# Loading batches 1 and 2 of q and k in 72 token runs: attention and a low-rank mixer on one Trainium2 core

## The chip, the cores and the metric

The kernel runs on one core of a Trainium2 chip. The metric is the time of one execution on the device in microseconds (us). Before the change the median of 8 executions is 364.96 us, the lowest 364.33, the highest 365.54.

## What is computed

Eight batches of eight heads, 576 tokens, 64 numbers per head. Attention is causal, with a bias from the running sum of a gate `s`; its output, heads side by side (512 wide), goes through a mixer over tokens of rank 32 and a two-layer network with a hidden width of 2048.

```python
scores = scale * np.matmul(q, k.transpose(0, 1, 3, 2))
s_pos = np.maximum(s, 0.0)
cum = np.cumsum(s_pos, axis=-1)
bias = -(cum[:, :, :, None] - cum[:, :, None, :])
scores = np.where(causal, -1000000000.0, scores + np.minimum(bias, 0.0))
attn = softmax(scores)
x = heads_side_by_side(np.matmul(attn, v))
u = x + (x.transpose(0, 2, 1) @ U @ V).transpose(0, 2, 1)
out = u + np.maximum(u @ w_ch1, 0.0) @ w_ch2
```

(The softmax and the joining of heads are shortened here to a name.)

## The kernel before

Work on q and k goes by pairs of heads. There are 32 pairs, four to a batch: pair n belongs to batch n // 4, so pairs 4 to 7 are batch 1 and pairs 8 to 11 batch 2. For each batch `alloc_qk` gives two tiles, `q_sd` and `k_sd`, each with 72 partitions, 8 heads and 8 x 64 numbers per head; the pool keeps two of each. `load_qk(b, h, n)` issues two loads, q and then k, for n heads from head h. They go out on POOL's queue, q0 in the profile, since they turn float32 into bf16 on the way.

The 576 tokens of a head are 72 x 8, and there are two ways to lay them over 72 partitions. In the first (L117) partition p holds tokens 8p to 8p + 7, so each partition and head is one run of 2 KB in memory. In the second (L112) partition p holds tokens p, p + 72, p + 144 and so on, so each token's 256 bytes are a run of their own. `in_runs(b, h)` chooses: true means the second.

`transposes(n)` then turns each head with eight matmuls against an identity (L315), two tokens' worth of 64 numbers at a time, into a PSUM tile `pwork` of bf16. Four copies per pair bring it to a `slot`, two per head: one for the even and one for the odd of each two. In the second layout a copy writes 72 neighbouring tokens at a time (L335). In the first it writes every second number, and reads PSUM with its last two dims swapped (L338). `copies` puts most of these copies on DVE; on ACT are all those of one head of pairs 4, 8 and 9, among others. The scores of pair n (`scores`, L402, with exponentials at L417, L428, L434 on ACT) read the slot; the values (`values`, L462, followed by L471 and L472 on DVE) read the exponentials and v.

The order of the work is written by hand. PE and POOL run in program order throughout (`in_program_order`); DVE, ACT and SP do so up to the end of batch 0, and behind that the order that the tile framework gives them holds. POOL's order at the start is: loads of batch 0, masks and constants, v of batch 0 in a form of its own, U and V, the first half of w1; the masks of pair 0; `load_qk(1, 0, 4)`; memsets; masks of pair 1; the second half of w1; masks of pairs 2 and 3; `load_qk(1, 4, 4)`; the first half of w2; v of batch 1 in five parts (L186); the second half of w2; q and k of batch 2 in two halves; v of batch 2; q and k of batch 3 whole, and so on. Batch 0 is loaded two heads at a time.

On PE, pairs 4 to 9 are woven together with the feed-forward matmuls of the first 512 tokens: L648 multiplies by w1, L658 by w2. In this string T is a step of `transposes`, S of `scores`, V of `values`, M of the mixer, F a step of the feed-forward alone:

```python
    weave("S5 T6 S5 F T6 S5 F S5 S6 T7 S6 T7 S6 S6")
    weave("V4 V4 S7 V5 S7 V5 S7 V6 S7 V6 T8 T8 V7 S8 V7 S8 T9 S8 T9")
```

The softmax here doesn't subtract the row's maximum and nothing guards it: scores larger than these inputs give would overflow.

## Time and profile before

| what | us |
|---|---|
| median of 8 executions | 364.96 |
| the profiled execution | 365.3 |
| its span, first to last instruction | 363.6 |
| PE busy in 35 to 80 us | 44.08 of 45 |
| L338 copies: DVE 29, ACT 11 | 23.3 busy on DVE |
| L112 issues on POOL, heads 4-7 of batch 2 | 1.42 and 1.40 each |
| L117 issues on POOL | 0.69 to 0.82 each |

The engines are PE (matmuls; PEld its weight loads), DVE, ACT, POOL and SP. A row of the profile gives line, engine, operation, tiles written and read, count, busy time, mean duration in ns, and the idle time before with what ended it. The strip of 40 digits shows the busy share of each fortieth of the span in tenths. q0 is the queue of the DMAs that POOL issues. [...]

### The profile page before, as it was taken

To read this page: it belongs to the slowest core of one execution; us is meant where nothing else is said; L and a number is where in the kernel's file an instruction comes from. 1 tells how busy PE (TensorE), PEld (TensorE's weight loads), DVE (VectorE), ACT (ScalarE), POOL (GpSimd) and SP (SyncE) were. 2 spreads that over 40 slices of the span, in tenths; PEclk is the share of its full clock that TensorE was granted. 3 is DMA by queue.
4 is the path that set the end of the run, shared out by engine and by line. 5 is a ranking of instruction groups with operands and counts; after the bars stand their busy time and mean duration, and the time that the engine had idled before them with its cause. 6 is when DMAs were issued, how large, how long until landed. Compare 5 with 4: busy or idle time off the path is not lost.

```text
span 363.6 us, 9585 instructions
## 1 busy us (share of the span) xinstructions
PE 351.4 (97%) x3989; PEld 255.2 (70%) x4031; DVE 278.5 (77%) x607; ACT 209.6 (58%) x319; POOL 85.0 (23%) x108
## 2 busy tenths in 40 slices
PE   7999999999999999999999999999999999999995
PEld 3676566666688667876688667876688468678884
DVE  7866776779798758995699659975899279676976
ACT  3884985746763678347843676357835641565710
POOL 8988452514040403140214012000000000000000
PEclk9999999999999999999999999999999999999999
DMA  7999999999999899989993999461013401500063
GB/s 102 171 202 198 165 182 102 153 144 131 112 61 101 137 143 60 99 92 125 127 99 66 144 134 90 50 165 23 18 49 88 96 18 32 147 0 31 29 117 116
DMA packets 153027, 37.41 MB, mean 103 GB/s; under 512 B 136600, under 2 KB 151352, under 8 KB 152984
## 3 DMA queue, kind: packets, MB, share of 16 engines
q0 software_dynamic: 110016, 18.50, 81.8%
q1 hardware_dynamic: 42680, 18.11, 28.9%
q8 instruction: 31, 0.51, 0.6%
q10 hardware_dynamic: 288, 0.20, 0.2%
q14 instruction: 12, 0.10, 0.1%
HBM read 37.25 MB, written 9.70 MB: 129 GB/s over the span
## 4 chain that ended last, share of the span: by engine, by line
PE 75%; DVE 12%; ACT 6%; issue 3%; DMA 2%; SPq 1%; DVEq 0%; ACTq 0%
PE pwork L648 24%; PE pwork L693 20%; PE pscore L402 9%; PE pwork L462 7%; PE parts L853 3%; PE pwork L315 3%; PE pwork L658 3%; DVE slot L675 2%; ACT hT L929 2%; DVE o_sb L707 2%; DVE uT L516 2%; ACT pT L417 2%; DMA slot<-hT 2%; PE pscore L648 1%; DVE slot L338 1%
## 5 line engine op out<-in xcount | busy, mean ns | idle before, releaser
L648 PE MATMUL pwork<-uT,w_sb 128*128 128x512 bf16 x431 | 113.8, 379 | 2.1 <-ACT hT L929 0.5
L417 ACT ACTIVATE pT<-pscore 128x1024 bf16<-128x1024 f32 x56 | 57.2, 1030 | 55.6 <-PE pscore L402 54.7
L929 ACT ACTIVATE hT<-pwork 128x512 bf16<-128x512 f32 x108 | 65.2, 609 | 31.2 <-PE pwork L648 31.1
L648 PEld LDWEIGHTS <-w_sb 128*128 128x128 bf16 x480 | 41.3, 98 | 37.3 <-issue 0.7
L402 PE MATMUL pscore<-slot 68*128 68x320 bf16 (+1 forms) x500 | 56.0, 246 | 0.7 <-DMA slot<-hT 0.5
L402 PEld LDWEIGHTS <-slot 68*128 68x128 bf16 x564 | 41.2, 97 | 17.5 <-issue 1.3
L693 PEld LDWEIGHTS <-hT 128*128 128x128 bf16 x496 | 46.1, 98 | 7.2 <-issue 0.7
L186 POOL DMA_DIRECT2D v_slot<-in_v_dram x36 | 30.3, 856 | 78.5 <-PE pwork L462 70.1
L693 PE MATMUL pwork<-w_sb,hT 128*128 128x256 bf16 x384 | 48.2, 273 | 0.0
L347 DVE TENSOR_TENSOR pT<-pT,keep 128x512 bf16<-128x512 bf16 (+1 forms) x81 | 28.6, 353 | 21.0 <-ACT pT L417 14.8
L335 DVE COPY slot<-pwork 64x576 bf16<-64x576 bf16 x76 | 34.4, 453 | 4.7 <-PE pwork L315 3.9
L462 PEld LDWEIGHTS <-pT 128*128 128x128 bf16 x870 | 32.4, 97 | 5.3 <-issue 0.6
L462 PE MATMUL pwork<-v_slot,pT 128*128 128x65 bf16 x870 | 35.5, 193 | 0.2 <-DVE uT L516 0.2
L693 PE MATMUL pwork<-w_sum,slot 128*128 128x256 bf16 x256 | 32.0, 273 | 0.8 <-DVE o_sb L707 0.7
L472 DVE TENSOR_TENSOR x_sb<-pwork,rec 128x320 bf16<-128x320 f32 x64 | 31.2, 488 | 1.3
L428 ACT ACTIVATE pT<-pscore 128x1024 bf16<-128x1024 f32 x29 | 30.2, 1042 | 2.6 <-PE pscore L402 2.4
L471 DVE RECIPROCAL rec<-pwork 128x5 f32<-128x5 f32 x64 | 12.1, 190 | 20.4 <-PE pwork L462 20.0
L338 DVE COPY slot<-pwork 64x576 bf16<-64x576 bf16 x29 | 23.3, 802 | 5.3 <-PE pwork L315 3.5
L693 PEld LDWEIGHTS <-slot 128*128 128x128 bf16 x256 | 24.1, 98 | 4.5 <-issue 1.6
L112 POOL DMA_DIRECT2D q_sd<-in_q_dram x6 | 12.6, 2105 | 47.6 <-PE pwork L315 42.2
L707 DVE TENSOR_TENSOR o_sb<-o_sb,pwork 128x512 f32<-128x512 f32 (+2 forms) x34 | 21.9, 648 | 0.7 <-PE pwork L693 0.3
L315 PEld LDWEIGHTS <-q_sd 72*128 72x128 bf16 x256 | 14.9, 97 | 8.9 <-DMA q_sd<-in_q_dram 1.1
(161 smaller groups left out, 500.1 us busy)
## 6 DMA issues: line engine op xcount, KB each, us to landing
out_dram<-o_sb SPq DMA_DIRECT2D x35, 256.0 KB
w_sb<-in_moe_w_ch_dram POOLq DMA_DIRECT2D x4, 1024.0 KB, 12.2
v_slot<-in_v_dram POOLq DMA_DIRECT2D x28, 128.0 KB, 6.7
q_sd<-in_q_dram POOLq DMA_DIRECT2D x5, 576.0 KB, 13.7
k_sd<-in_k_dram POOLq DMA_DIRECT2D x5, 576.0 KB, 17.9
q_sd<-in_q_dram POOLq DMA_DIRECT2D x4, 288.0 KB, 12.6
k_sd<-in_k_dram POOLq DMA_DIRECT2D x4, 288.0 KB, 11.4
q_sd<-in_q_dram POOLq DMA_DIRECT2D x4, 144.0 KB, 4.8
```

The source lines that it names most:

```text
L186: nc.gpsimd.dma_start(out=vt[:rows_t, t, :, 0:D], in_=v[b, :, ds(t * 128, rows_t), :].rearrange("h p d -> p h d"),)
L335: copies(n, hh, par)(by_run[:, :, :, par, :], src)
L347: nc.vector.tensor_tensor(dst, dst, keep[:, :, 0:w].to_broadcast([128, n_tiles, w]), op=ALU.min)
L402: nc.tensor.matmul(dst, lhsT=slot[0:KA, hh, ds(S + j * 128, 128)], rhs=slot[0:KA, hh, lo:hi], start=True, stop=True,)
L417: nc.scalar.activation(pT[:, hh, 0:1024], near, EXP, scale=scale)
L428: nc.scalar.activation(pT[:, :, 1024:1536], mid.rearrange("p (a b) -> p a b", a=2), EXP, scale=scale)
L462: nc.tensor.matmul(po[:, i, :], lhsT=pT[:, hh, ds(place(j, i), 128)], rhs=vt[:, j, h, :], start=(j == 0), stop=(j == i), skip_group_check= ...
L472: nc.vector.tensor_tensor(x_sb[:, hp, :, ds(hh * D, D)], po[:, :, 0:D], rec.to_broadcast([128, 5, D]), op=ALU.mult,)
L648: nc.tensor.matmul(f1, lhsT=w1_sb[:, kt, ds(nf * 128, 128)], rhs=u[:, kt, :], start=(kt == 0), stop=(kt == 3),)
L693: nc.tensor.matmul(acc[:, i, :], lhsT=a[:, kt, ds(i * 128, 128)], rhs=b[:, kt, :], start=(i == 0 and kt == 0), stop=(kt == HF - 1), skip_g ...
L707: nc.vector.tensor_tensor(dst, a, b, op=ALU.add)
L929: nc.scalar.activation(hT[:, nf, :], f1, RELU)
```

## The change

`in_runs` is true for every batch but batch 0, where before it was true from the second half of batch 2 on. So the loads of q and k for all of batch 1 (two pairs of loads of four heads) and for the first half of batch 2 (one pair) take the second layout, and the copies of pairs 4 to 9 take the form of L335.

```diff
     def in_runs(b, h):
-        return b > 2 or b == 2 and h >= 4
+        return b > 0
```

PE's instructions stand in the same order as before, and so do POOL's, where only the form of the six loads differs. On DVE some copies of pairs 5 to 7 and the copies into V_sb and V_end change places with their neighbours, and on SP one of the small row loads (L299).

## The prediction

> **What bounds the kernel now.** I read the page first: busy shares, the slices, then the two copy rows.

> ```profile
> PE 351.4 (97%) x3989; PEld 255.2 (70%) x4031; DVE 278.5 (77%) x607; ACT 209.6 (58%) x319; POOL 85.0 (23%) x108
> DMA  7999999999999899989993999461013401500063
> q0 software_dynamic: 110016, 18.50, 81.8%
> L335 DVE COPY slot<-pwork 64x576 bf16<-64x576 bf16 x76 | 34.4, 453 | 4.7 <-PE pwork L315 3.9
> L338 DVE COPY slot<-pwork 64x576 bf16<-64x576 bf16 x29 | 23.3, 802 | 5.3 <-PE pwork L315 3.5
> ```

> PE is busy for 97% of the span, and the DMA engines have almost no free slice in the first third. So two things run without a pause where the change acts: PE's instruction stream, and q0, the queue of the loads that POOL issues. The table by stage says how much PE loses there (columns: stretch, then busy time and count of PE, PEld, DVE, ACT, POOL, then clock, DMA share, GB/s):

> ```profile
> 35.00:80.00 45.00, 44.08 (x530) 28.57 (x536) 32.38 (x69) 32.99 (x48) 18.90 (x20) 1.00 2.62 152
> ```

> In 45 us PE idles 0.92 us. PE's order is fixed by hand, so nothing done in that stretch by DVE or ACT can give back more than this. The timeline names the waits in it that the old copies end, and the transposes of pair 8, the first reader of batch 2:

> ```profile
> 53.48 1.14 PE L462 MATMUL pwork<-v_slot,pT 128*128 128x65 bf16 x30
> 54.88 1.02 PE L658 MATMUL pwork<-w_sb,hT 128*128 128x512 bf16 x4 [0.26 <-DVE slot L338]
> ...
> 61.76 0.30 PE L315 MATMUL pwork<-identity,q_sd 72*128 72x72 bf16 x4
> 61.89 0.29 PE L315 MATMUL pwork<-identity,k_sd 72*128 72x72 bf16 x4
> ...
> 63.88 0.34 PEld L402 LDWEIGHTS <-slot 68*128 68x128 bf16 x6 [0.24 <-ACT slot L338]
> ```

> Last, POOL's timeline, and beside it the time from issue to landing, read one issue at a time (last number, us). The first five lines below are issues (start, duration); the next four are the landings of w_sb at 35.71, k_sd at 41.57, q_sd at 42.95 and k_sd at 44.37:

> ```profile
> 35.71 0.89 POOL L273 DMA_DIRECT2D w_sb<-in_moe_w_ch_dram  x1 [1.27 <-DMA q_sd<-in_q_dram]
> 36.97 0.75 POOL L117 DMA_DIRECT2D q_sd<-in_q_dram  x1 [0.37 <-PE pwork L648]
> 41.57 0.72 POOL L117 DMA_DIRECT2D k_sd<-in_k_dram  x1 [3.85 <-PE pwork L648]
> 42.95 1.42 POOL L112 DMA_DIRECT2D q_sd<-in_q_dram  x1 [0.67 <-issue]
> 44.37 1.40 POOL L112 DMA_DIRECT2D k_sd<-in_k_dram  x1
> ...
> w_sb<-in_moe_w_ch_dram POOLq DMA_DIRECT2D x1, 1024.0 KB, 15.6
> k_sd<-in_k_dram POOLq DMA_DIRECT2D x1, 288.0 KB, 13.1
> q_sd<-in_q_dram POOLq DMA_DIRECT2D x1, 288.0 KB, 16.1
> k_sd<-in_k_dram POOLq DMA_DIRECT2D x1, 288.0 KB, 16.6
> ```

> Issue plus landing gives w_sb 51.3, k_sd of the first half of batch 2 at 54.7, its second half at 59.1 (q) and 61.0 (k). Loads land in the order of issue, each right after the one before: q0 is a full pipe, and a load made longer pushes back all later ones. The same sum over the other issues gives the table that I work with: w1 first half 24.2; q, k of batch 1, heads 0-3: 25.8, 27.5; w1 second half 32.9; q, k heads 4-7: 35.4, 36.4; w2 first half 41.0; v of batch 1 (five parts) 42.0 to 47.0; w2 second half 51.3; q, k of batch 2, heads 0-3: 53.6, 54.7; heads 4-7: 59.1, 61.0; v of batch 2: 67.6; q, k of batch 3: 72.6, 79.3.

> **The change part by part.** *Copies.* 24 of the 40 L338 copies (pairs 4 to 9, four each) become L335 copies; PE's and POOL's orders stay, and on DVE a few copies move ahead of a neighbouring mask. 18 are on DVE: 18 x (802 - 453 ns) = 6.3 us of DVE time. 6 are on ACT, where L338 takes 799 and L335 634 ns (medians of the two lines): 1.0 us. On the path this is worth only what PE waits for: 0.26 us at 54.88 and 0.24 at 63.88, 0.5 in all; the bound is the 0.92 of the stage, the other bound nothing. PE's matmuls cover the rest, and cover it still if those copies were slow.

> *POOL.* The six issues go from about 0.73 us (L117) to 1.41 (the L112 rows above, same tile): 6 x 0.68 = 4.1 us. Behind the first two (17.15 and 17.91) stand the masks of pairs 1 to 3, the memset of slot rows and the issue of w1's second half. All shift by 1.4 us. The masks of pair 3 end at 26.44 now after waits of 0.15 and 0.57 us for ACT; these take up half of the shift, so they end near 27.1. Their reader, the values of pair 3, starts on PE at 27.75. Price: nothing, with 0.65 us of cover; without it each further 0.1 us of POOL is 0.1 of PE. The other issues have only memsets and further issues behind them, and q0 has 10 us of work in hand then. Two issues wait for landings: w_sb at 35.71 (for q_sd's, at 35.4) and k_sd at 41.57 (the page names PE, long done; w2's first half landed at 41.0). They will go out some 6 us later, at about 42 and 47, still before the pipe is through v of batch 1 (near 53). No gap, so no price. SP's queue is untouched.

> *The pipe.* Each pair of q and k loads of four heads is now 2 x 288 runs, and becomes 2 x 2304 runs of one token: 4608 instead of 576 packets, and 12096 more in all three pairs. The old pair takes 27.5 - 24.2 = 3.3, 36.4 - 32.9 = 3.5 and 54.7 - 51.3 = 3.4 us of the pipe: 3.4. The new form stands in the trace once at the same size: heads 4-7 of batch 2, 61.0 - 54.7 = 6.3 us. Other rows for 4608 packets of 128 B: q and k of batch 3, (79.3 - 67.6) / 2 = 5.9; v of batch 1, 47.0 - 41.0 = 6.0; batch 4 under other traffic, k issued at 85.49 and landed 17.9 later, at 103.4, less 86.0 where v of batch 3 (issued 73.84, 12.2 to landing) ended, halved, 8.7. The fastest stretch is this:

> ```profile
> DMA packets 2991, 0.39 MB, mean 156 GB/s; under 512 B 2977, under 2 KB 2991, under 8 KB 2991
> ```

> That is 40.0 to 42.5: 1191 a us, or 3.9 us for 4608. So a pair costs 0.5 to 5.3 us more; I take the row of the same shape, 6.3 - 3.4 = 2.9.

> [...] The row says a factor of 1.85, and I go by the row.

> Now each reader against its load, with 2.9 us per pair passed. Pair 6 reads k at 44.19: 36.4 + 5.8 = 42.2, in time. The values of pair 4 start at 53.48 and read v's last part at about 53.9: 47.0 + 5.8 = 52.8, in time by 1.1. The output matmuls on w2's second half start at 58.84: 51.3 + 5.8 = 57.1, in time. Pair 8 reads k at 61.89: 54.7 + 8.7 = 63.4. **Late by 1.5 us.** It turns so from 61.9 - 54.7 = 7.2 us, that is 2.4 per pair, a pair price of 5.8. PE's order is fixed, so all behind it waits: an output group, the rest of pair 8, values of pair 7. That the copies freed PE at 54.88 is lost in front of this wait, since a landing ends it. The 0.24 us at 63.88 is still won. Later readers: batch 2's second half 69.7 against pair 10 at 78.24; v 76.3 against values of pair 8 at 79.63; batch 3's k 88.0 against pair 12 near 89.7, which is itself 1.3 later by then. In time.

> Sum: +1.5 - 0.24 = +1.3 us. The profiled execution took 365.3 us with a span of 363.6; the median shown is 364.96, which I add to: 366.2.

> **Rivals.** *A, the forecast: pair 8 waits.* Bounds from prices of 5.9 to 6.8: late by 0.3 to 3.0, so 365.0 to 367.7. For it: the row of the same shape and source. Against it: that row lies where packets of q, k and v mix, the two pairs of batch 1 where they don't.

> *B, the pipe keeps up.* At the fast rate (0.5 more a pair) up to 2.4, nothing waits, and what counts is the copies: -0.5, at most -0.92, taken as -0.7 with small waits the page doesn't list: 364.3. For it: 1191 packets a us were seen just there, with v of batch 1. Against it: no q or k load in this form came near it.

> *C, the pipe is much slower.* With the price of batch 4 (5.3 more), v of batch 1 lands at 57.6 and holds values of pair 4 by 3.7 us, and pair 8's k at 70.6 comes 8.7 late in all: 364.96 + 8.7 - 0.24 = 373.4; half way between A and C, 369.8. For it: POOL, DVE and SP traffic are all at work. Against it: batch 4's loads shared the engines with output and transposes, which hardly run before 62 us.

> That the copies don't change form is excluded: every L338 copy of pairs 4 to 9 turns into L335 in the new order.

> **How the numbers follow.** A 0.47, B 0.38, C 0.15. About 0.2%, 0.73 us, is what a measurement of this kernel can tell from no change. C and 0.40 of A are slower: 0.55. The edge of A, 0.07, and 0.13 of B are within. The rest of B, 0.25, is faster. The range runs from B's bound (364.96 - 0.92) to about half way to C, 364.0 to 370.0; A's own is 365.0 to 367.7.

> **What would show it.** q0 at 122112 packets; POOL near 89 us; DVE near 272; 16 L338 copies left; k_sd of batch 2 landing near 63.4; an idle PE of about 1.5 us at L315 released by DMA k_sd near 62 (A); none there and no L338 wait (B); waits at L462 near 54 too (C). I am wrong in kind if PE waits for POOL's masks near 27, or for a load of batch 3 or later.

## The result, and the profile after

The changed kernel takes 367.99 us (median of 21; lowest 365.90, highest 371.90), beside 364.70 before (median of 58): a ratio of 1.0087, 95% interval 1.007 to 1.0104. It is slower, by 3.2 us (0.0087 x 364.7) where 1.3 was forecast; the forecast range of 364.0 to 370.0 holds the time. The profiled execution took 369.7 us, 1.7 above the median, with a span of 368.0, 4.4 above the span of before.

From the page of the changed kernel, busy shares, q0, and the row of the unit-step copies on DVE:

```profile
PE 352.8 (96%) x3989; PEld 256.6 (70%) x4031; DVE 272.3 (74%) x607; ACT 208.7 (57%) x319; POOL 88.8 (24%) x108
q0 software_dynamic: 126144, 18.52, 93.8%
L335 DVE COPY slot<-pwork 64x576 bf16<-64x576 bf16 x94 | 42.6, 453 | 9.4 <-PE pwork L315 8.4
```

DVE lost 6.2 us of work and POOL gained 3.8, as the change says. PE is busy for 1.4 us more and idle for about 3 more. The table of PE's waits says where (who waited for whom, us in total, times, longest):

```profile
PE pwork L462 <- DVE uT L516: 2.4, 1, 2.4
PE pwork L315 <- DMA k_sd<-in_k_dram: 1.5, 1, 1.5
PE pwork L462 <- issue: 1.4, 1, 1.4
```

No wait for an L338 copy of pairs 4 to 9 is left. Three waits stand out, and PE's timeline places them. The second line below is pair 8, the place of the forecast wait:

```profile
29.54 0.19 PE L462 MATMUL pwork<-v_slot,hT 128*128 128x65 bf16 x1 [1.35 <-issue]
...
61.41 0.29 PE L315 MATMUL pwork<-identity,k_sd 72*128 72x72 bf16 x4
...
90.56 0.30 PE L315 MATMUL pwork<-identity,k_sd 72*128 72x72 bf16 x4 [1.50 <-DMA k_sd<-in_k_dram]
...
118.85 0.98 PE L462 MATMUL pwork<-v_slot,pT 128*128 128x65 bf16 x15 [2.44 <-DVE uT L516]
```

Pair 8 was just in time here. Pair 12, the first of batch 3, waited 1.5 us for its k. The values of pair 12, at 118.85, waited for DVE, and DVE's own timeline says for what:

```profile
114.61 0.68 DVE L707 TENSOR_TENSOR o_sb<-U,pwork 128x512 f32<-128x512 f32 x1
117.44 0.56 DVE L516 TENSOR_TENSOR uT<-pwork,xT 128x384 bf16<-128x384 f32 x1 [2.16 <-DMA xT<-x_sb]
```

xT is x turned by a DMA transpose that SP issues (L479). DVE adds it to a product in a PSUM bank, and PE waited for that bank. So a queue that the change never touched was late. And PE came out of this wait at half its clock (last columns: PEclk, DMA share, GB/s):

```profile
112.00:116.10 4.10, 4.01 (x43) 3.33 (x41) 2.93 (x8) 0.57 (x2) 0.00 (x0) 1.00 1.58 84
118.80:122.20 3.40, 3.35 (x39) 2.81 (x39) 2.25 (x6) 0.00 (x0) 0.00 (x0) 0.50 0.24 81
```

The start of the write of x_sb (L472) for a head marks how far PE is. Taken from both timelines, after less before, it accounts for the whole span of this execution:

```
up to        before   after    difference   what lies between
pair 3 h0     28.64   27.97      -0.67      chance at the start
pair 3 h1     29.86   30.00      +0.14      +0.81  gap near 28 us
pair 9 h0     89.48   88.68      -0.80      -0.94  the new copies
pair 10 h0    96.04   96.69      +0.66      +1.46  k of batch 3
pair 13 h0   125.34  129.79      +4.44      +3.78  transposes of x, and the half clock
pair 31 h0   290.09  294.54      +4.46      nothing more
```

Why the loads were late is seen in the landings of the k loads issued at 18.39, 28.04, 45.83 and 70.35 in the changed kernel (last number, us from issue):

```profile
k_sd<-in_k_dram POOLq DMA_DIRECT2D x1, 288.0 KB, 11.1
k_sd<-in_k_dram POOLq DMA_DIRECT2D x1, 288.0 KB, 12.8
k_sd<-in_k_dram POOLq DMA_DIRECT2D x1, 288.0 KB, 15.3
k_sd<-in_k_dram POOLq DMA_DIRECT2D x1, 576.0 KB, 20.2
```

They land at 29.5, 40.8, 61.1 and 90.5, against 27.5, 36.4, 54.7 and 79.3: late by 2.0, 4.4, 6.4 and 11.2 us. The lateness grows by about 2.1 us with each of the three pairs, and then by nearly 5 more up to the k of batch 3, 4.3 of them inside batch 3, whose loads the change leaves alone (v of batch 2 landed 6.9 us late, at 74.5).

### The profile page after: what moved, and what is told of

The parts are those of the page before. It is cut to its first block, busy times and chain, and to the rows that moved or that the text cites. A ratio compares the mean times of both kernels' runs of the same rounds, so it can differ in the third digit from the quotient of the medians.

```text
span 368.0 us, 9584 instructions
## 1 busy us (share of the span) xinstructions
PE 352.8 (96%) x3989; PEld 256.6 (70%) x4031; DVE 272.3 (74%) x607; ACT 208.7 (57%) x319; POOL 88.8 (24%) x108
## 3 DMA queue, kind: packets, MB, share of 16 engines
q0 software_dynamic: 126144, 18.52, 93.8%
## 5 line engine op out<-in xcount | busy, mean ns | idle before, releaser
L648 PE MATMUL pwork<-uT,w_sb 128*128 128x512 bf16 x431 | 113.8, 379 | 2.1 <-ACT hT L929 0.5
L417 ACT ACTIVATE pT<-pscore 128x1024 bf16<-128x1024 f32 x56 | 57.1, 1027 | 58.8 <-PE pscore L402 58.0
L648 PEld LDWEIGHTS <-w_sb 128*128 128x128 bf16 x480 | 41.3, 98 | 37.0 <-issue 0.7
L402 PE MATMUL pscore<-slot 68*128 68x320 bf16 (+1 forms) x500 | 56.0, 246 | 0.1
L402 PEld LDWEIGHTS <-slot 68*128 68x128 bf16 x564 | 41.3, 97 | 16.7 <-issue 1.3
L335 DVE COPY slot<-pwork 64x576 bf16<-64x576 bf16 x94 | 42.6, 453 | 9.4 <-PE pwork L315 8.4
L693 PE MATMUL pwork<-w_sb,hT 128*128 128x256 bf16 x384 | 49.1, 276 | 0.0
L347 DVE TENSOR_TENSOR pT<-pT,keep 128x512 bf16<-128x512 bf16 (+1 forms) x81 | 28.7, 355 | 24.2 <-ACT pT L417 16.2
L462 PE MATMUL pwork<-v_slot,pT 128*128 128x65 bf16 x870 | 36.2, 195 | 2.5 <-DVE uT L516 2.4
L462 PEld LDWEIGHTS <-pT 128*128 128x128 bf16 x870 | 33.1, 99 | 7.7 <-issue 2.9
L472 DVE TENSOR_TENSOR x_sb<-pwork,rec 128x320 bf16<-128x320 f32 x64 | 31.2, 488 | 1.3
L112 POOL DMA_DIRECT2D q_sd<-in_q_dram x9 | 17.0, 1884 | 51.3 <-PE pwork L315 37.3
L315 PEld LDWEIGHTS <-q_sd 72*128 72x128 bf16 x256 | 15.1, 98 | 8.7 <-DMA q_sd<-in_q_dram 0.9
L315 PE MATMUL pwork<-identity,k_sd 72*128 72x72 bf16 x256 | 18.0, 198 | 1.5 <-DMA k_sd<-in_k_dram 1.5
## 6 DMA issues: line engine op xcount, KB each, us to landing
w_sb<-in_moe_w_ch_dram POOLq DMA_DIRECT2D x4, 1024.0 KB, 15.8
q_sd<-in_q_dram POOLq DMA_DIRECT2D x4, 288.0 KB, 14.5
k_sd<-in_k_dram POOLq DMA_DIRECT2D x4, 288.0 KB, 12.8
```

The costliest lines, as they stand in the source:

```text
L315: nc.tensor.transpose(tps[hh][:, c, t2, :], src[:, 2 * hp + hh, ds(t2 * 128, 128)], identity[:TP, :TP],)
L335: copies(n, hh, par)(by_run[:, :, :, par, :], src)
L347: nc.vector.tensor_tensor(dst, dst, keep[:, :, 0:w].to_broadcast([128, n_tiles, w]), op=ALU.min)
L402: nc.tensor.matmul(dst, lhsT=slot[0:KA, hh, ds(S + j * 128, 128)], rhs=slot[0:KA, hh, lo:hi], start=True, stop=True,)
L417: nc.scalar.activation(pT[:, hh, 0:1024], near, EXP, scale=scale)
L462: nc.tensor.matmul(po[:, i, :], lhsT=pT[:, hh, ds(place(j, i), 128)], rhs=vt[:, j, h, :], start=(j == 0), stop=(j == i), skip_group_check= ...
```

## The experiments

The theory after this reading: the copies gain 0.9 us, everything lost comes from the pipe of loads being late, in three places (the gap near 28 us, k, the transposes of x), and a long wait costs PE's clock besides (0.50 for 3.4 us behind the wait of 2.44). Medians below are beside 364.8 to 365.0 us of the kernel before, run on the same chip in the same set. Most differ from the changed kernel by the condition in `in_runs` alone.

### Copies alone, loads alone

`in_runs` here decides the loads alone, and `in_unit_steps` the copies:

```diff
     def in_runs(b, h):
+        return b > 2 or b == 2 and h >= 4
+
+    def in_unit_steps(b, h):
         return b > 0
...
-                if in_runs(b, 2 * hp):
+                if in_unit_steps(b, 2 * hp):
```

> Loads as before the change (2 KB runs for batch 1 and the first half of batch 2), copies of pairs 4 to 9 in the new form of L335. The tokens of those pairs then stand in permuted places of the slots, so this kernel leaves the right order of tokens out and is read for its time alone. Theory (the copies are worth what PE waited for, and every loss comes from the queue of loads): 0.5 to 0.95 us faster than before, ratio 0.9974 to 0.9986, no PE wait on a load of q or k, gap at the last value matmul of pair 3 near 28 us as before (0.5 us). Rival (the new copies, or DVE's changed order, cost something themselves): no change or slower.

Measured: 363.88 us, ratio 0.998 (0.9951 to 1.001), profiled span 362.0. The interval holds 1, so the gain in the median, 0.92 us, is shown by the profile rather than by the ratio: between pair 3 and pair 9 PE's marks move from -0.68 to -1.62 us, the same 0.94 as in the changed kernel, and no load of batch 1 or later is waited for. The gap near 28 us is 0.44.

PE's row of 35 to 80 us, with which the prediction bounds this gain, reads so in a later profile of the kernel before, and with the copies alone (columns as in the prediction):

```profile
35.00:80.00 45.00, 44.61 (x527) 28.35 (x525) 32.45 (x71) 32.52 (x48) 19.25 (x21) 1.00 2.47 156
35.00:80.00 45.00, 45.00 (x540) 28.80 (x539) 28.04 (x72) 32.52 (x49) 18.88 (x20) 1.00 2.59 154
```

So PE idles 0.39 us there, and 0.40 in one more profile, not 0.92. The profile that the prediction read has 3989 matmul records where these have 4031; in its stretch of 45 us ten records are missing, and each leaves a hole of some 0.05 us that looks idle. The gain is more than the 0.39 all the same. Matmul by matmul, four steps from one start to the next shrink with the new copies, by 0.13, 0.07, 0.43 and 0.29 us, 0.93 in all. The 0.43 is the wait that the row at 54.88 puts at 0.26: PE starts these value matmuls every 29 ns while the profile draws each 193 ns long, so the row hides the first 0.16 us of the wait.

With the two conditions swapped:

> Loads in 72 token runs as in the changed kernel, copies of pairs 4 to 9 in the old form of L338. The tokens of those pairs stand in permuted places, so the right order of tokens is left out. Theory: the whole loss without the gain: slower than the changed kernel by 0.5 to 0.95 us, that is 3.5 to 4.5 us slower than before (ratio 1.010 to 1.012), but only where waits on loads do not swallow the difference: a wait that a landing ends hides a PE that is late anyway, and then it is equal to the changed kernel (1.0087). Rival (copies matter more than PE's waits say): over 1.5 us slower than the changed kernel.

Measured: 366.99 us, ratio 1.0072 (1.0047 to 1.0097). It isn't slower than the changed kernel. The numbers expected were wrong; the reason given for the exception fits this profile. PE, 0.57 us behind the kernel of before at pair 9 where the changed kernel is 0.80 ahead, waited for no load of batch 1 or later (pair 12 read its k at 90.25, and k had landed at 89.5) and 0.94 us for the transposes. So what the copies win in front of a late landing is lost in waiting for it. That k landed 1.0 us earlier here than in the changed kernel's profile helped as well.

### Batch 3, then batch 4, back in 2 KB runs

```diff
-        return b > 0
+        return b > 0 and b != 3
```

> The changed kernel, but batch 3 is loaded in 2 KB runs (and its copies take the old form): q0 carries 8064 packets less between 70 and 90 us, with batches 1 and 2 as late as in the changed kernel. Theory (the lateness of the queue is carried to batch 3's k and to the transposes of x near 115 us): the 1.5 us wait at pair 12 and the 2.4 us wait at 116 us are both gone, the gap of 1.35 us near 28 us stays; 363.9 to 365.2 us against 364.7 before. Rival (those waits come from POOL's later issues or from the DMA transposes themselves): both waits stay, and the time is that of the changed kernel, near 368.

Measured: 366.61 us, ratio 1.0057 (1.0034 to 1.0079). A miss in the time, half a hit in the places. Pair 12 no longer waits, and the wait for the transposes is 0.62. But in this execution pair 8 waits, just as forecast:

```profile
63.12 0.30 PE L315 MATMUL pwork<-identity,k_sd 72*128 72x72 bf16 x4 [1.53 <-DMA k_sd<-in_k_dram]
```

Its k was issued at 46.69 and took 16.4 us: landed at 63.1, 8.4 us later than before the change, where the changed kernel's profile has 6.4 for the same loads. With the loads alone changed, the same k landed 7.1 us late. The lateness differs by 2 us between profiles with the same loads up to there, and pair 8 stands right on the edge.

```diff
-        return b > 0
+        return b > 0 and b != 4
```

> The changed kernel, but batch 4 (loaded between 84 and 114 us) in 2 KB runs, with its copies in the old form. Batches 1 to 3 are as in the changed kernel. Theory (the wait near 116 us is for the DMA transposes of x, which share the 16 engines with batch 4's runs when these come late): the wait at the values of pair 12 falls from 2.4 to 0.2 us and PE's clock does not fall behind it; the gap near 28 us stays (1.2 to 1.8 us), and so does a wait of 0 to 1.6 us for a k load, at pair 8 or pair 12; 365.0 to 366.4 us. Rival (the transposes are late because they were issued late, or for a cause of their own): the wait at 116 us stays over 0.5 us, time near 367 to 368.

Measured: 369.68 us, ratio 1.0134 (1.009 to 1.0178). The wait for the transposes is gone (0.19 us, as before the change). PE was also 3.15 us behind the kernel before by then, which alone would hide a wait, but the transposes themselves were fast again: the last of the four was issued at 109.96 and landed 5.5 us later by its semaphore, as before the change (5.6) and unlike the changed kernel (10.0). Thirteen profiles show where batch 4's k landed: in the six where that was by 107.7 us this transpose took 5.3 to 5.6 us, in the seven where it was from 108.5 on, 7.4 to 10.0. So these transposes were slow where they met batch 4's late runs. The time is a miss: pair 8 waited 0.51, pair 12 longer than ever, and the clock fell there instead:

```profile
91.62 0.30 PE L315 MATMUL pwork<-identity,k_sd 72*128 72x72 bf16 x4 [1.99 <-DMA k_sd<-in_k_dram]
...
92.70:96.10 3.40, 3.40 (x24) 2.05 (x23) 1.09 (x3) 1.43 (x3) 0.00 (x0) 0.50 3.10 109
```

From pair 9 to pair 10 PE's marks move by 3.6 us, 2.0 of which is the wait.

### Lateness with no short packet

To the kernel before, two loads that nobody reads, behind the first half of batch 2:

```diff
+            if b == 2 and h == 0:
+                one = work.tile([128, 4, 640], BF16, tag="xT", name="xT", bufs=1)
+                nc.gpsimd.dma_start(out=one, in_=w1_in[:, :, 0:640])
...
+                nc.gpsimd.dma_start(
+                    out=two.rearrange("p a b c -> p a (b c)"), in_=w1_in[:, :, 0:512]
+                )
```

> The kernel before the change, all loads and copies as they were, with two loads more behind the first half of batch 2 (1280 and 1024 bytes a packet, 1.15 MB in bf16, nobody reads them): the pipe is late by some 6 us from there on, with no short packet added and nothing late at pair 8. Theory (it is the lateness of the pipe that is paid, further on, and not the number of short packets): k of batch 3 lands near 86 to 90, a wait at pair 12 of 0 to 1.5 us, one of 0.4 to 2.4 at the values of pair 12 near 116 us, gap near 28 us as before (0.4 to 0.6): 365.2 to 368 us. Rival (short packets between 24 and 60 us are what costs): no wait, 364.5 to 365.0 us.

Measured: 365.33 us, ratio 1.0019 (0.9989 to 1.0049), which can't be told from no change; of 12 times 7 lie between 364.5 and 365.6 and 3 between 366.6 and 367.1; the others are 368.9 and 522.1. The profiled execution, 366.9, is of the second kind. k of batch 3 was issued at 68.04 and landed 20.7 later, at 88.7, in time; the transposes were not:

```profile
117.61 0.61 PE L462 MATMUL pwork<-v_slot,pT 128*128 128x65 bf16 x15 [1.44 <-DVE uT L516]
```

So lateness alone, made by packets of 1 KB and over, brings back the wait for the transposes of x. It takes no more short packets than before the change.

### One pair at a time

```diff
-        return b > 0
+        return b > 2 or b == 2 and h >= 4 or b == 1 and h < 4
```

> Of the three pairs of loads only the first, heads 0 to 3 of batch 1, is changed, with its copies. Theory on the gap near 28 us (4032 more packets beside the fetch of PE's code make the fetch late): the gap is 1.2 to 1.5 us as in the changed kernel and not 0.54; q0 is some 2 us late afterwards, so no PE wait on a load of batch 3; the copies of pairs 4 and 5 hardly counted: 365.2 to 365.9 us against 364.7. Rival (the gap is a chance of the one profiled execution): gap of 0.5 us, and a time within 0.5 us of before.

Measured: 365.13 us, ratio 1.0026 (1.0 to 1.0052); gap near 28 us 1.64 us. The wait at 54.88 for an L338 copy is still there.

Only the second pair:

> Only the second pair of loads (heads 4 to 7 of batch 1) is changed, with the copies of pairs 6 and 7. Theory: as for the third pair alone, pipe 2 us late behind 36 us, no wait for a load, gap near 28 us as before; the copy of pair 7 in front of the wait at 54.88 us is worth 0.25 to 0.45 us: 364.2 to 364.6 us. Rival (any lateness of the pipe is paid at 116 us): 365 to 366.

Measured: 364.15 us, ratio 0.9983 (0.9953 to 1.0013), the lowest median of all that keep the tokens in order, though the interval doesn't part it from the kernel before. Nothing waits for a load, and the wait at 54.88 is gone.

Only the third:

> Only the third pair of loads (heads 0 to 3 of batch 2) is changed, with the copies of pairs 8 and 9. Theory: the pipe is 2 to 3 us late behind 54 us, nothing waits for a load, gap near 28 us as before; gain of the copies on ACT and DVE 0.2 to 0.4 us: 364.3 to 364.7 us against 364.7 to 364.8. Rival (any lateness of the pipe is paid at 116 us): 365 to 366.

Measured: 364.32 us, ratio 0.999 (0.9962 to 1.0018). As expected, and as little settled by its interval.

The second and the third:

> The first pair of loads (heads 0 to 3 of batch 1) goes back to 2 KB runs with old copies for pairs 4 and 5; the second and the third pair stay changed. Theory: the fetch of code near 27 us takes some 0.95 to 1.0 us and not 1.4 to 2.1, the gap near 28 us is 0.4 to 0.55; the pipe is later by 4 us and not 6.4 at batch 2's first half, so pair 8 does not wait; batch 3's k lands near 85 to 88, just before pair 12 reads it at 88.8; batch 4's end near 108 to 110, so the wait at 116 us is 0.2 to 0.6; copies worth 0.6 to 0.9: 363.9 to 365.2 us. Rival (the loss of the change comes from the later pairs): over 366.

Measured: 366.40 us, ratio 1.0033 (0.9998 to 1.0067), a miss on the rival's side, and two kinds of times: four of twelve from 363.6 to 364.9, eight from 366.2 to 368.9. Its profile was of the first kind, span 362.0, with no wait for a load. The same kernel once more:

> The second and third pair changed once more, for its profile: of its 12 times before, 4 were under 365 and 8 over 366 us, and the profile was of the first kind. Theory (where the pipe's landing comes after pair 12's or the transposes' reader, PE waits, and a wait of 2 us or more also halves its clock for 3.4 us): a profile of the slower kind shows a wait of over 1.5 us at pair 12 or near 116 us, with a stretch of half clock behind it. A profile of the faster kind shows none, and tells nothing new.

Measured: one execution, 367.18 us, of the second kind:

```profile
116.34 0.91 PE L462 MATMUL pwork<-v_slot,pT 128*128 128x65 bf16 x15 [2.08 <-DVE uT L516]
...
116.00:120.00 4.00, 3.66 (x41) 3.09 (x41) 2.92 (x9) 0.00 (x0) 0.00 (x0) 0.57 0.26 72
```

Up to pair 11 it was 1.51 us ahead of the kernel before, from pair 13 on 1.97 behind: 3.5 us for a wait of 2.1. That parts this execution from the one of the first kind. It need not be what all eight slower ones lost: six of them, from 366.2 to 366.9, had a granted clock of 0.998 or 1.0, so hardly a stretch at half clock, and no profile shows their waits.

A trade, two pairs earlier in runs and the second half of batch 2 back:

```diff
-        return b > 0
+        return b > 2 or b == 2 and h < 4 or b == 1 and h >= 4
```

> Second and third pair of loads in 72 token runs (pairs 6 to 9 copied in unit steps), the second half of batch 2 back in 2 KB runs (pairs 10 and 11 copied as before): one pair of loads more in runs than before the change, and not two or three. Theory: pipe late by 2 to 3 us behind 61 us, no wait for a load, gap near 28 us as before, copies worth 0.5 to 0.9 us at pairs 7 and 8, and the old copies of pairs 10 and 11 cost nothing or up to 0.3: 363.8 to 364.4 us, and no bimodal times as with the second and third pair changed. Rival (DVE is tight near 80 us, when pairs 10 and 11 are copied): 364.7 or more.

Measured: 365.59 us, ratio 1.0007 (0.998 to 1.0034). A miss: pair 8 waited 0.92 us, since its k landed at 61.9, late by 7.2 us with two pairs changed, and PE later lost 0.6 us to DVE near 91. In the two profiles with only the second and third pair changed, where the loads ahead of this k are the same, it was late by 5.0.

### The gap near 28 us

PE stops at the last value matmul of pair 3 with nothing to wait for that the profile names. In the same microseconds one packet of 16 KB passes on q8, the queue that the page names `instruction`; whose code it holds the profile does not say. Its time is its share of 16 engines' time in a stretch of 1.5 us, before the change and after:

```profile
q8 instruction: 1, 0.02, 4.0%
```

```profile
q8 instruction: 1, 0.02, 6.7%
```

4.0% of 24 us is 0.96 us, 6.7% is 1.6.

> The changed kernel with the second half of w1 issued ahead of the first pair of loads: the same packets, but the runs of batch 1 pass the pipe at about 29 to 35 us and not at 24 to 30. Theory on the gap near 28 us (PE's code is fetched at 26 us beside these runs): that fetch takes 0.9 to 1.05 us again and the gap is 0.4 to 0.6 us; instead pair 4 may wait for its k at 35 us, by up to 1 us, and the fetch near 33 us is slower; the rest as in the changed kernel, so 367 to 368 us. Rival (the gap comes from the copies or from POOL's later masks): it stays at 1.2 to 1.8.

The change here is one line moved: the issue of w1's second half goes ahead of the first pair of loads. Measured: 370.18 us, ratio 1.0112 (1.0065 to 1.0159), above the range expected. The code packet took 0.94 us and the gap was gone; pair 4 waited 1.0 us for q and 1.22 for k in its place, pair 8 0.64, pair 12 1.21 and the values of pair 12 2.40.

But the kernel with the two spare loads had a gap of 1.46 us without short packets at that point. So the kernel with the first pair alone changed, and the kernel before, each ran twice more:

> The kernel with the first pair of loads alone changed, for its profile. Theory (runs beside the fetch of PE's code lengthen the gap near 28 us): fetch of 1.4 to 2.1 us and a gap of 1.2 to 1.8 us. Rival (the gap varies by itself): a fetch of under 1.1 us or a gap under 0.7.

> As the kernel with the first pair alone changed: theory, a gap of 1.2 to 1.8 us near 28 us; rival, under 0.7.

> The kernel before the change, for a second profile of it. Theory: fetch near 27 us of 0.9 to 1.05 us and a gap of 0 to 0.65 us. Rival (the gap varies by itself, as in the kernel with the two spare loads, 1.46 us with a fetch of 0.95): over 1.2 us.

> The kernel before the change, a third profile of it: theory, a gap of 0 to 0.65 us near 28 us; rival, over 1.2.

Measured: gaps of 0.95 and 1.15 us with the first pair changed, 0.17 and 0.27 in the kernel before; times 364.95 and 364.96 against 364.26 and 364.80. Over all profiles the seven with the first pair in short runs have code packets of 1.40 to 2.09 us and gaps of 0.95 to 1.79, mean 1.36. The eleven others have packets of 0.93 to 1.00 us and gaps of 0 to 0.64, but for that one of 1.46, mean 0.43. The two sets of packet times don't overlap. That short packets lengthen the code packet's time is shown; that this makes the whole of the gap is not, since the gap can be long without.

## Why the prediction was right in direction and too small

**Copies: right in place, too small in size.** Taken at 0.24 us on the path, with 0.92 as the bound. Measured 0.94, in the changed kernel and with the copies alone. That this meets the bound is chance: over half of the 0.92 were holes of missing records, and the steps that the copies shortened lay partly under matmuls that the profile draws as busy. The 0.24 at 63.88 is a row of PEld; PE's own step there shrank by 0.29. The loss of the gain at 54.88 "in front of this wait" didn't happen at pair 8 in the profiled execution; it happened further on.

**The pipe: right.** 2.9 us a pair was taken, 2.1 measured in the changed kernel. Over three pairs it came to 6.4 there and 7.1, 7.2 and 8.4 in three others with the same loads, against 8.7 forecast. The row of the same shape was a little dear.

**Pair 8: a matter of the execution.** Forecast late by 1.5 us, turning at a lateness of 7.2. It waited 1.53, 0.92, 0.64 and 0.51 us in four of the experiments' profiles, and not in the changed kernel's. So the one term that made the forecast slower measured nothing in the profile, and that the direction came out right there is luck: other terms, which stood at nothing, made it so.

**The step that failed is "Later readers".** The forecast carried the same 8.7 us on to batch 3's k, put it at 88.0 against pair 12 at 89.7 "which is itself 1.3 later by then", and said in time. k landed at 90.5, and PE stood ready at 88.9, early by the copies: a wait of 1.5 us. The loads of batch 3 were priced at the 11.7 us that they took before; pushed back, they took 16.0. In those 16.0 us q0 moved 1.20 MB, about what it moved in the 11.7 of before (1.24), and q1, the queue of the transfers that SP issues, 1.19 MB against 0.56. That fits a pipe that shares its engines with SP's transposes and output; it was not tested by itself. The prediction said that it would be wrong in kind if PE waited for a load of batch 3, and so it was.

**"SP's queue is untouched" was true of its issues only, and failed with it.** The transfers of that queue were late all the same: a transpose landed 10.0 us behind its issue, where it was 5.6 before. The wait for the transposes of x, 2.4 us, is the largest single wait, and no rival had it. Batch 4 back in 2 KB runs removes it, spare loads bring it back.

**Two costs were not in the sum at all**: the half clock behind a long wait, some 1.5 us, and the longer gap beside the code packet, +0.81 in the profile and +0.9 in the means. The half clock is not in every execution: a stretch of 3.4 us at half clock takes the mean granted clock of a run to 0.995, and nine of the 22 on record have 0.997 or more. These nine have a median of 366.7 us.

**Small steps.** POOL at 88.8 us (89 forecast), DVE 272.3 (272), 16 L338 copies left, as forecast; the masks of pairs 1 to 3 cost PE nothing, which was the forecast with 0.65 us of cover. q0 has 126144 packets, not 122112: the other 4032 are of 4 bytes.

## What to carry to other kernels

When a queue has no pause, follow a lateness until the queue next runs empty, re-price every load that now meets other traffic, and count among its readers the transfers of other queues that run beside it: here a transpose took 10.0 us and not 5.6, and a code packet 1.60 and not 0.95. What faster copies gave an engine that is 97% busy was near its waits (0.94 us) and far from the 6.3 us of work saved. But the idle sum of a profile is no exact bound on it: count the records, and compare the starts of the same matmuls in two kernels. And where readers stand on the edge, ask what a wait costs beyond itself (here up to 1.6 us).

## What the runs showed of the hardware

The code packet of 16 KB near 27 us took 0.93 to 1.00 us in the eleven profiles without the first pair's short runs beside it and 1.40 to 2.09 in the seven with runs of 128 bytes. The six loads added 16128 packets to q0, 12096 for their runs and 4032 of 4 bytes. The lateness of the same loads varied by 2 us between profiles, and the changed kernel's times spread over 6 us.
